# Earlier loads of batch 3, one scaling for both groups of batch 1, and a reordered opening

## The chip, the cores and the metric

The kernel runs on one core of a Trainium2 chip. The time is the device time of one execution in microseconds (us). Five runs of the kernel before gave a median of 313.35 us, from 313.18 to 313.67.

The engines are named as the profile names them: PE (matrix products; PEld are its weight loads), DVE (vector), ACT (scalar functions), POOL and SP. SP computes nothing here and issues most of the DMA transfers; POOL issues those that change the type, and casts v.

## The reference

Two stages. A linear attention over 8 batches, 8 heads, 576 positions and a head size of 64, then a gated feed-forward layer on the 4608 tokens that come out of it (width 512, hidden width 1536):

```python
q_s = np.exp(q - max(q, axis=-1));  q_s = q_s / sum(q_s, axis=-1)
k_s = np.exp(k - max(k, axis=2));   k_s = k_s / sum(k_s, axis=2)
kv  = einsum('bhsd,bhse->bhde', k_s, v)
x   = einsum('bhsd,bhde->bhse', q_s, kv)      # then (batch, position, head*64)
g   = x @ w_gate
out = (g * sigmoid(g) * (x @ w_val)) @ w_out
```

Inputs and output are float32. The kernel computes in bfloat16 with float32 sums. It takes no maximum, and it divides by the sum of k after the product K^T V rather than before.

## The kernel before

**Attention.** A batch is worked on as two groups G of four heads. For each group: `exp_of` (ACT) makes eq and ek; `norm_sum` and `norm_mul` (DVE) divide eq by its row sums and give qs; qs is turned, giving qt, either by PE (`turn_pe`, then a copy `turn_out`) for batches 0 and 1, or by a DMA transpose on SP's queue (`turn_dma`, L178) for the others. `cast_v` (POOL, L122) writes v in bfloat16 beside a column of ones, so `kv_mm` (L187), 72 products of 64x64 over both groups, gives K^T V and the sum of k at once. Scaling by the reciprocal of that sum gives kn. The x product (`x_mm` for batch 0, `x_and_next_kv` for the others, L242) multiplies kn with qt, and ACT and DVE copy the result from PSUM into xt (L256, L257).

**Feed-forward.** The tokens go in chunks: 576 of batch 0, then 448, then 512 each. `m_unit` makes 128 of the 1536 hidden values for a chunk: eight (or sixteen) products with w_gate and w_val (L281), a silu on ACT (L288) and a product on DVE (L289). `o_mm` multiplies hidden values with w_out (L306) for 128 tokens in twelve steps m; `o_out` copies the result to an o_sb buffer and stores it in two halves (L299) on SP's queue.

**What sets the order.** The order on each engine is written out by hand, and every engine works through its own list in order. PSUM has eight banks, handed out as they come free. The tiles for loaded q, k and v have three buffers each (`ld`), ek, eq, qs and qt two (`at`), o_sb five. A load into a buffer in use waits at the head of SP's queue, with everything behind it.

**Around the change.** In the opening, batch 0 is turned, multiplied and copied while the first weight slices are on their way. Then come the loads of batches 1 and 2 on SP, then the first chunk's twelve `m_unit`, and then a stretch in which `o_mm` of the first tokens fills PE between the steps of batch 1's attention. There K^T V of batch 1 has two banks for each group, and each group's half is scaled by its own reciprocal (L482) and product (L483):

```python
for G in range(NG):
    kv_mm(1, G, kv[G], 0)
    for g in range(2):
        kvr = at.tile([128, 1], FP32, tag=f"kvr{g}", name="kvr")
        nc.vector.reciprocal(out=kvr, in_=kv[G][g][:, 64:65])
        nc.vector.tensor_scalar_mul(kn[:, g, G], kv[G][g][:, 0:64], kvr)
```

Later batches use two banks for both groups (columns 0 and 256 of each) and `scale_both` (L227, L228). Batch 3's loads stand at the end of this stretch, behind the stores of the first four outputs and ahead of batch 2's first transpose. Batch 2's x product follows in the second chunk, after its eleventh `m_unit`, together with batch 3's K^T V.

Of the kernel before, what the change touches and what calls it, by code (L numbers as in the profile page):

```python
# [8 lines left out]
FP32 = mybir.dt.float32  # L9
BF16 = mybir.dt.bfloat16  # L10
# [5 lines left out]
def kernel(  # L16
# [10 lines left out]
    nc = tc.nc  # L27
# [8 lines left out]
    NG = H // 4  # L36
# [5 lines left out]
    at = ctx.enter_context(tc.tile_pool(name="at", bufs=2))  # L42
# [4 lines left out]
    def bank(name):  # L47
        return psp.tile([128, 512], FP32, tag="ps", name=name)
# [16 lines left out]
    def head_ap(src, b, G, t0=0, t1=T):  # L65
        return bass.AP(
            tensor=src.tensor,
            offset=src[b, 4 * G].offset + 64 * t0,
            ap=[[T * 64, 128], [2 * HSTR, 2], [1, (t1 - t0) * 64]],
        )  # L70

    def load(what, src, b, G, pieces=((0, T),), after=None):
        t_ = ld.tile([128, 2, T * 64], FP32, tag=what, name=what)
        raw[what, b, G] = t_
        last = None
        for t0, t1 in pieces:
            last = nc.sync.dma_start(out=t_[:, :, 64 * t0:64 * t1], in_=head_ap(src, b, G, t0, t1))  # L77
            if after is not None:
                tc.add_manual_dep(last.ins, after.ins.name, SYNC, reason="order of loads")
                after = None  # L80
        return last

    def load_kv(b):
        for G in range(NG):
            load("k", k, b, G)
            load("v", v, b, G)
# [17 lines left out]
    def copy(eng, out, in_):  # L104
        if eng is nc.scalar:
            nc.scalar.copy(out=out, in_=in_)  # L106
        else:
            eng.tensor_copy(out=out, in_=in_)  # L108
# [3 lines left out]
    st = {}  # L112

    def exp_of(what, b, G, pieces=((0, T),)):
        s = st.setdefault((b, G), {})
        e = s["e" + what] = at.tile([128, T, 2, 64], BF16, tag="e" + what, name="e" + what)
        src = raw[what, b, G].rearrange("p h (t d) -> p t h d", d=64)
        for t0, t1 in pieces:
            nc.scalar.activation(out=e[:, t0:t1], in_=src[:, t0:t1], func=AF.Exp)  # L119
# [34 lines left out]
    def turn_pe(b, G, i):  # L154
        s = st[b, G]
        if i == 0:
            s["qt"] = at.tile([128, T, 128], BF16, tag="qt", name="qt")
        t0, t1 = BANKS[i]
        tp = s["tp", i] = psp.tile([128, 1024], BF16, tag="ps", name="tp")
        for t in range(t0, t1):  # L160
            j = t - t0
            nc.tensor.transpose(  # L162
                out=tp[:, j * 128:(j + 1) * 128], in_=s["qs"][:, t, :], identity=ident
            )

    def turn_out(b, G, i, eng):
        s = st[b, G]
        t0, t1 = BANKS[i]
        copy(
            eng,  # L170
            s["qt"][:, t0:t1, :],
            s["tp", i][:, 0:(t1 - t0) * 128].rearrange("p (t c) -> p t c", c=128),
        )
# [8 lines left out]
    def kv_mm(b, G, kv, c):  # L182
        ek = st[b, G]["ek"]
        for t in range(T):
            for g in range(2):
                for h in range(2):
                    nc.tensor.matmul(  # L187
                        out=kv[g][HALF[h], c:c + 65], lhsT=ek[HALF[g], t, h, :],
                        rhs=vbs[G][HALF[g], t, h, :],
                        start=(t == 0), stop=(t == T - 1),  # L190
                    )

    def x_mm(b, G, i):
        s = st[b, G]
        t0, t1 = BANKS[i]
        xp = [bank("xp") for _ in range(2)]
        for g in range(2):
            for h in range(2):
                r = slice(64 * h, 64 * h + 64)
                nc.tensor.matmul(  # L200
                    out=xp[h][64 * g:64 * g + 64, 0:64 * (t1 - t0)],
                    lhsT=s["kn"][r, g, :],
                    rhs=s["qt"][r, t0:t1, 64 * g:64 * g + 64],
                    start=True, stop=True,
                )
        return xp

    def x_out(b, G, i, xp, engs=(nc.scalar, nc.vector)):
        t0, t1 = BANKS[i]
        n = 64 * (t1 - t0)  # L210
        c0 = b * S + 64 * t0
        for h in (h for h in range(2) if engs[h] is not None):
            copy(engs[h], xt[:, 2 * G + h, c0:c0 + n], xp[h][:, 0:n])
# [1 line left out]


    def kv_both(b):
        kv = st["kv", b] = [bank("kv") for _ in range(2)]
        for G in range(NG):
            kv_mm(b, G, kv, 256 * G)  # L220

    def scale_both(b):
        kn = st["kn", b] = at.tile([128, 2, NG, 64], BF16, tag="kn2", name="kn2")
        for g in range(2):
            kv = st["kv", b][g].rearrange("p (G c) -> p G c", c=256)
            kvr = at.tile([128, NG], FP32, tag=f"kvrr{g}", name="kvr")
            nc.vector.reciprocal(out=kvr, in_=kv[:, :, 64])  # L227
            nc.vector.tensor_mul(kn[:, g], kv[:, :, 0:64], kvr.to_broadcast([128, NG, 64]))  # L228
# [72 lines left out]
    def o_mm(j, o_ps=None, m0=0, m1=MT):  # L301
        if o_ps is None:
            o_ps = bank("o_ps")
        r0 = (j * 128) % RING
        for m in range(m0, m1):
            nc.tensor.matmul(  # L306
                out=o_ps, lhsT=hr[:, m, r0:r0 + 128], rhs=wo[:, m, :],
                start=(m == 0), stop=(m == MT - 1),
            )
        return o_ps  # L310

    def o_out(j, o_ps, eng=nc.vector):
        o_sb = osb.tile([128, 512], FP32, tag="o_sb", name="o_sb")
        copy(eng, o_sb, o_ps)
        store(j, o_sb)
# [20 lines left out]
    with tc.manual_schedule():  # L336
# [50 lines left out]
        def kv_first(G, t0=0, t1=T):  # L387
            s = st[0, G]
            if t0 == 0:
                s["kv"] = [bank("kv") for _ in range(2)]  # L390
            for t in range(t0, t1):
                for g in range(2):
                    for h in range(2):
                        nc.tensor.matmul(
                            out=s["kv"][g][HALF[h], 0:64], lhsT=s["ek"][HALF[g], t, h, :],
                            rhs=v16[G][HALF[g], h, 64 * t:64 * t + 64],
                            start=(t == 0), stop=(t == T - 1),
                        )

        def scale_first(G, eng1):  # L400
            s = st[0, G]
            kn = s["kn"] = at.tile([128, 2, 64], BF16, tag="kn1", name="kn1")
            nc.scalar.mul(kn[:, 0, :], s["kv"][0][:, 0:64], s["kvr"][:, 0:1])
            if eng1 is nc.scalar:
                nc.scalar.mul(kn[:, 1, :], s["kv"][1][:, 0:64], s["kvr"][:, 1:2])
            else:
                nc.vector.tensor_scalar_mul(kn[:, 1, :], s["kv"][1][:, 0:64], s["kvr"][:, 1:2])
# [12 lines left out]
        key_sum(1)  # L420
        scale_first(0, nc.scalar)
        turn_pe(0, 1, 0)
        turn_out(0, 1, 0, nc.vector)
        xp0 = x_mm(0, 0, 0), x_mm(0, 0, 1)
        turn_pe(0, 1, 1)
        turn_out(0, 1, 1, nc.vector)
        kv_first(1, *BANKS[0])
        kv_first(1, *BANKS[1])
        x_out(0, 0, 0, xp0[0], (nc.scalar, None))
        x_out(0, 0, 1, xp0[1], (nc.scalar, None))  # L430
        scale_first(1, nc.vector)
        x_out(0, 0, 0, xp0[0], (None, nc.scalar))
        x_out(0, 0, 1, xp0[1], (None, nc.vector))
        xp1 = x_mm(0, 1, 0), x_mm(0, 1, 1)
        x_out(0, 1, 0, xp1[0])
        x_out(0, 1, 1, xp1[1])
# [7 lines left out]
        for what, src in (("q", q), ("k", k), ("v", v)):  # L444
            for G in range(NG):
                load(what, src, 2, G)

        for m in range(MT):
            m_unit(0, S, m, by_group=(m == 0))
# [21 lines left out]
        turn_pe(1, 1, 1)  # L471
        turn_out(1, 1, 0, nc.scalar)
        turn_out(1, 1, 1, nc.vector)
        kv = [[bank("kv") for _ in range(2)] for _ in range(NG)]
        p3 = o_mm(3, m1=6)
        o_out(2, p2)
        kn = st["kn", 1] = at.tile([128, 2, NG, 64], BF16, tag="kn2", name="kn2")
        for G in range(NG):
            kv_mm(1, G, kv[G], 0)
            for g in range(2):  # L480
                kvr = at.tile([128, 1], FP32, tag=f"kvr{g}", name="kvr")
                nc.vector.reciprocal(out=kvr, in_=kv[G][g][:, 64:65])  # L482
                nc.vector.tensor_scalar_mul(kn[:, g, G], kv[G][g][:, 0:64], kvr)  # L483
        exp_of("q", 2, 0)
        o_mm(3, p3, m0=6, m1=9)
        x_and_next_kv(1, with_kv=False)
        o_mm(3, p3, m0=9)
        o_out(3, p3)
        exp_of("q", 2, 1)
        norm_sum(2, 0)  # L490
# [3 lines left out]
        exp_of("k", 2, 1)  # L494
        cast_v(2, 0)
        cast_v(2, 1)
        load_kv(3)
        turn_dma(2, 0)

        chunks = [(S, 448)] + [(c, 512) for c in range(1024, n_tok, 512)]  # L500
        for ci, (c0, n) in enumerate(chunks):
            b = ci + 2
# [84 lines left out]
```

The softmax here doesn't subtract the row's maximum and nothing guards it: scores larger than these inputs give would overflow.

## Time and profile before

| | |
|---|---|
| median of the runs | 313.35 us |
| the profiled execution | 313.33 us |
| its span, first to last instruction | 311.2 us |
| PE, DVE, ACT, POOL busy | 302.0, 161.2, 146.7, 33.2 us |
| granted PE clock | 1.00 |
| DMA moved, mean rate | 45.78 MB, 147 GB/s |

The profile is one execution. Busy time is given by engine; instructions that only wait, branch or issue a DMA don't count as busy, and those of a queue are named with a q (SPq). A row of the timeline gives start and length in us, engine, line, operation, what is written and read, and in brackets how long the engine was idle before it and what it then waited for. The chain is followed back from the last instruction, at each step to what released it. Lengths of matmuls include their pipeline, so the distance between starts says more than the length.

### The profile page before, as it was taken

What the parts mean: (1) busy time and instruction counts of PE and PEld (TensorE: products, weight loads), DVE (VectorE), ACT (ScalarE), POOL (GpSimd) and SP (SyncE); (2) the same over time, 40 slices, a digit from 0 to 9 for tenths busy, and PEclk for the clock granted to TensorE, in tenths of its full rate; (3) what the DMA queues carried; (4) which work ended last, traced back from release to release, by engine and by line L of the source; (5) the groups of instructions that cost most, each with busy time, mean ns of one, the idle gap of its engine ahead of it and who ended that gap; (6) DMA issues with size and microseconds to landing.
All of it is one profiled execution on the core that took longest, in us unless ns stands there. A gap on an engine that the chain in (4) does not pass through costs nothing.

```text
span 311.2 us, 5454 instructions
## 1 busy us (share of the span) xinstructions
PE 302.0 (97%) x2182; PEld 149.4 (48%) x2182; DVE 161.2 (52%) x277; ACT 146.7 (47%) x215; POOL 33.2 (11%) x39
## 2 busy tenths in 40 slices
PE   6889999999999999999999999999999999999994
PEld 2567845545444444454444444444444444444442
DVE  3834478936763567355836492639354333333321
ACT  5843478794764465547364637455143113312300
POOL 2960021420200110002000200000000000000000
PEclk9999999999999999999999999999999999999999
DMA  7999999899355906491629253605310302020134
GB/s 279 181 193 204 277 386 389 292 236 379 106 100 150 373 17 132 91 376 61 143 62 354 110 108 69 189 0 106 65 42 0 70 8 60 3 67 8 25 70 103
DMA packets 41690, 45.78 MB, mean 147 GB/s; under 512 B 18496, under 2 KB 25664, under 8 KB 41664
## 3 DMA queue, kind: packets, MB, share of 16 engines
q1 hardware_dynamic: 32752, 39.99, 43.5%
q0 software_dynamic: 8752, 5.31, 12.0%
q8 instruction: 17, 0.28, 0.4%
q10 hardware_dynamic: 160, 0.13, 0.1%
q14 instruction: 9, 0.07, 0.1%
HBM read 37.75 MB, written 9.44 MB: 152 GB/s over the span
## 4 chain that ended last, share of the span: by engine, by line
PE 93%; DMA 4%; POOL 1%; issue 0%; SPq 0%; DVE 0%
PE g_ps L281 30%; PE u_ps L281 30%; PE o_ps L306 29%; DMA wg<-in_moe_w_gate_dram 2%; DMA k<-in_k_dram 2%; PE xp L242 2%; PE kv L187 2%; PE o_ps L326 1%; POOL v L344 0%; PE tp L162 0%; POOL v L341 0%; POOL wg L94 0%; POOL wv L94 0%; SPq L77 0%; DVE o_sb L330 0%
## 5 line engine op out<-in xcount | busy, mean ns | idle before, releaser
L288 ACT ACTIVATE sg<-g_ps 128x512 bf16<-128x512 f32 (+2 forms) x120 | 64.7, 555 | 134.9 <-PE g_ps L281 133.1
L289 DVE TENSOR_TENSOR hr<-sg,u_ps 128x512 bf16<-128x512 bf16 (+2 forms) x120 | 74.2, 630 | 89.0 <-PE u_ps L281 82.5
L281 PE MATMUL g_ps<-xt,wg 128*128 128x512 bf16 (+2 forms) x480 | 111.4, 358 | 0.9 <-DMA wg<-in_moe_w_gate_dram 0.9
L281 PE MATMUL u_ps<-xt,wv 128*128 128x512 bf16 (+2 forms) x480 | 111.3, 358 | 0.0
L306 PE MATMUL o_ps<-wo,hr 128*128 128x512 bf16 x420 | 93.9, 379 | 0.0
L281 PEld LDWEIGHTS <-wv 128*128 128x128 bf16 x480 | 46.9, 98 | 46.4
L281 PEld LDWEIGHTS <-wg 128*128 128x128 bf16 x480 | 46.2, 98 | 46.5 <-DMA wg<-in_moe_w_gate_dram 1.2
L306 PEld LDWEIGHTS <-hr 128*128 128x128 bf16 x420 | 40.9, 98 | 48.5
L108 DVE COPY o_sb<-o_ps 128x512 f32<-128x512 f32 x33 | 22.5, 681 | 39.2 <-PE o_ps L306 39.2
L122 POOL CAST vb<-v 128x1152 bf16<-128x1152 f32 x14 | 18.3, 1308 | 134.6 <-DMA v<-in_v_dram 123.0
L133 DVE TENSOR_REDUCE rs<-eq 128x18 f32<-128x1152 bf16 (+2 forms) x18 | 21.7, 1215 | 12.9 <-ACT eq L119 12.9
L147 DVE TENSOR_TENSOR qs<-eq,rr 128x1152 bf16<-128x1152 bf16 (+2 forms) x18 | 21.7, 1216 | 0.1
L119 ACT ACTIVATE eq<-q 128x1152 bf16<-128x1152 f32 (+2 forms) x18 | 18.3, 1052 | 4.0 <-DMA q<-in_q_dram 3.9
L119 ACT ACTIVATE ek<-k 128x1152 bf16<-128x1152 f32 (+2 forms) x17 | 18.1, 1102 | 0.3 <-DMA k<-in_k_dram 0.2
L288 ACT ACT_TABLE_LOAD x12 | 15.4, 1283 | 0.2
L119 ACT ACT_TABLE_LOAD x11 | 14.1, 1283 | 0.2
L256 ACT CAST xt<-xp 128x512 bf16<-128x512 f32 x14 | 7.9, 587 | 4.5 <-PE xp L242 4.4
L371 PE MATMUL idle<-zero 128*128 128x512 bf16 x20 | 6.3, 467 | 3.0 <-DVE rs L133 1.8
L257 DVE CAST xt<-xp 128x512 bf16<-128x512 f32 x14 | 9.0, 683 | 0.0
L242 PE MATMUL xp<-qt,kn 64*64 64x512 bf16 (+1 forms) x112 | 7.2, 293 | 0.0
L187 PEld LDWEIGHTS <-ek 64*64 64x64 bf16 x504 | 6.3, 107 | 1.7 <-ACT qt L106 0.4
L187 PE MATMUL kv<-vb,ek 64*64 64x65 bf16 x504 | 6.8, 194 | 0.0
(45 smaller groups left out, 63.3 us busy)
## 6 DMA issues: line engine op xcount, KB each, us to landing
q<-in_q_dram SPq DMA_DIRECT2D x16, 576.0 KB, 5.5
out_dram<-o_sb SPq DMA_DIRECT2D x70, 128.0 KB, 2.4
k<-in_k_dram SPq DMA_DIRECT2D x15, 576.0 KB, 7.3
v<-in_v_dram SPq DMA_DIRECT2D x14, 576.0 KB, 8.5
wo<-in_moe_w_out_dram POOLq DMA_DIRECT2D x4, 384.0 KB, 14.3
wg<-in_moe_w_gate_dram POOLq DMA_DIRECT2D x2, 384.0 KB, 10.6
wv<-in_moe_w_val_dram POOLq DMA_DIRECT2D x2, 384.0 KB, 11.8
wg<-in_moe_w_gate_dram POOLq DMA_DIRECT2D x2, 256.0 KB, 7.7
```

Of the source, the lines that this page charges most:

```text
L108: eng.tensor_copy(out=out, in_=in_)
L119: nc.scalar.activation(out=e[:, t0:t1], in_=src[:, t0:t1], func=AF.Exp)
L122: return nc.gpsimd.tensor_copy(out=vbs[G][:, :, :, 0:64], in_=raw["v", b, G].rearrange("p h (t d) -> p t h d", d=64),)
L133: i = nc.vector.reduce_sum(out=rs[:, 2 * t0:2 * t1], in_=eq2[:, 2 * t0:2 * t1, :], axis=mybir.AxisListType.X)
L147: last = eng.tensor_mul(qs[:, t0:t1, :].rearrange("p t (h d) -> p (t h) d", d=64), eq2[:, 2 * t0:2 * t1, :], s["rr"][:, 2 * t0:2 * t1].to_ ...
L187: nc.tensor.matmul(out=kv[g][HALF[h], c:c + 65], lhsT=ek[HALF[g], t, h, :], rhs=vbs[G][HALF[g], t, h, :], start=(t == 0), stop=(t == T - 1),)
L242: nc.tensor.matmul(out=o[h][HALF[g], c:c + 64 * (t1 - t0)], lhsT=kn[HALF[h], g, G, :], rhs=qt[G][HALF[h], t0:t1, 64 * g:64 * g + 64], star ...
L257: nc.vector.tensor_copy(out=xt[:, 2 * G + 1, c0:c0 + 512], in_=main[G][1])
L281: nc.tensor.matmul(out=gu[a][i][:, 0:w_], lhsT=(wg, wv)[a][:, kk, ms], rhs=xt[:, kk, c:c + w_], start=(kk == 0), stop=(kk == KT - 1),)
L288: nc.scalar.activation(out=sg[:, 0:w_], in_=g_ps[:, 0:w_], func=AF.Silu)
L289: nc.vector.tensor_mul(hr[:, m, r:r + w_], sg[:, 0:w_], u_ps[:, 0:w_])
L306: nc.tensor.matmul(out=o_ps, lhsT=hr[:, m, r0:r0 + 128], rhs=wo[:, m, :], start=(m == 0), stop=(m == MT - 1),)
```

## The change

There are three edits. In the opening, the two PE transposes of group 1 stand together ahead of the x product of group 0, and the copies of that product to xt are dealt out differently: group 0's first half (h = 1) goes to DVE instead of ACT, and ACT's copy of the second bank pair (h = 0) stands behind the scaling of group 1 instead of ahead of it. In the stretch after the first chunk, K^T V of batch 1 is put into two banks for both groups and scaled by `scale_both`, and five instead of three `o_mm` steps of the fourth output stand between it and the x product. Three of batch 3's four loads move from behind the first outputs' stores to a place right behind batch 2's loads.

```diff
     def kv_both(b):
-        kv = st["kv", b] = [bank("kv") for _ in range(2)]
+        if ("kv", b) not in st:
+            st["kv", b] = [bank("kv") for _ in range(2)]
         for G in range(NG):
-            kv_mm(b, G, kv, 256 * G)
+            kv_mm(b, G, st["kv", b], 256 * G)
...
         turn_pe(0, 1, 0)
+        turn_pe(0, 1, 1)
         turn_out(0, 1, 0, nc.vector)
+        turn_out(0, 1, 1, nc.vector)
         xp0 = x_mm(0, 0, 0), x_mm(0, 0, 1)
-        turn_pe(0, 1, 1)
-        turn_out(0, 1, 1, nc.vector)
         kv_first(1, *BANKS[0])
         kv_first(1, *BANKS[1])
         x_out(0, 0, 0, xp0[0], (nc.scalar, None))
-        x_out(0, 0, 1, xp0[1], (nc.scalar, None))
         scale_first(1, nc.vector)
-        x_out(0, 0, 0, xp0[0], (None, nc.scalar))
-        x_out(0, 0, 1, xp0[1], (None, nc.vector))
+        x_out(0, 0, 0, xp0[0], (None, nc.vector))
+        x_out(0, 0, 1, xp0[1])
...
             for G in range(NG):
                 load(what, src, 2, G)
+        load("k", k, 3, 0)
+        load("v", v, 3, 0)
+        load("k", k, 3, 1)
...
-        kv = [[bank("kv") for _ in range(2)] for _ in range(NG)]
+        st["kv", 1] = [bank("kv") for _ in range(2)]
         p3 = o_mm(3, m1=6)
         o_out(2, p2)
-        kn = st["kn", 1] = at.tile([128, 2, NG, 64], BF16, tag="kn2", name="kn2")
-        for G in range(NG):
-            kv_mm(1, G, kv[G], 0)
-            for g in range(2):
-                kvr = at.tile([128, 1], FP32, tag=f"kvr{g}", name="kvr")
-                nc.vector.reciprocal(out=kvr, in_=kv[G][g][:, 64:65])
-                nc.vector.tensor_scalar_mul(kn[:, g, G], kv[G][g][:, 0:64], kvr)
+        kv_both(1)
+        scale_both(1)
         exp_of("q", 2, 0)
-        o_mm(3, p3, m0=6, m1=9)
+        o_mm(3, p3, m0=6, m1=11)
         x_and_next_kv(1, with_kv=False)
-        o_mm(3, p3, m0=9)
+        o_mm(3, p3, m0=11)
         o_out(3, p3)
...
         cast_v(2, 1)
-        load_kv(3)
+        load("v", v, 3, 1)
         turn_dma(2, 0)
```

## The prediction

> **What bounds the kernel now.** I read the page's busy times and chain first, then the waits, then the timeline of each engine around the three places that the diff touches. PE is busy for nearly the whole span, and the chain that ended last is PE almost throughout.
>
> ```profile
> PE 302.0 (97%) x2182; PEld 149.4 (48%) x2182; DVE 161.2 (52%) x277; ACT 146.7 (47%) x215; POOL 33.2 (11%) x39
> PE 93%; DMA 4%; POOL 1%; issue 0%; SPq 0%; DVE 0%
> ```
>
> So an edit pays only if it closes a gap in PE's stream, and costs only if it opens one. From the timelines of PE and of its weight loads, these are the gaps near the edits (start, length, what, idle before it):
>
> ```profile
> 17.27 1.15 PE L281 MATMUL g_ps<-xt,wg 128*128 128x320 bf16 x8 [0.92 <-DMA wg<-in_moe_w_gate_dram]
> ...
> 50.65 0.11 PEld L242 LDWEIGHTS <-kn 64*64 64x64 bf16 x4 [0.42 <-DVE kvr L482]
> 50.98 0.11 PEld L242 LDWEIGHTS <-kn 64*64 64x64 bf16 x2 [0.23 <-DVE kn L483]
> 51.38 0.35 PEld L242 LDWEIGHTS <-kn 64*64 64x64 bf16 x10 [0.29 <-DVE kn L483]
> ```
>
> The first is the opening: unit m=1 of the first chunk waits for a slice of w_gate. The other three are batch 1's x product waiting for the scaled K^T V. From 52.4 us to the last chunks single matmuls follow each other at their own pace (0.19 or 0.216 us), so nothing else is there to win. The other reading that matters is SP's queue, and who needs it (SP, then PE, then the group of the transposes: shortest, median, longest in ns):
>
> ```profile
> 48.58 8.36 SPq L299 DMA_DIRECT2D out_dram<-o_sb  x8
> 58.72 0.58 SPq L77 DMA_DIRECT2D v<-in_v_dram  x1
> 59.41 8.09 SPq L178 DMA_TRANSPOSE qt<-qs  x2
> ...
> 70.02 0.41 PE L242 MATMUL xp<-qt,kn 64*64 64x512 bf16 x4
> ...
> L178 SPq DMA_TRANSPOSE qt<-qs x12: 1275/1343/4252, 59.4 to 217.9; - x12
> ```
>
> The two transposes of batch 2 land at 68.48 and 69.50; PE uses them at 70.02 and 70.58. That is the tightest thing downstream: 1.5 and 1.1 us.
>
> **Part 1, the opening.** Nothing is added; four transposes move ahead of the x product, and one copy of 128x320 goes from ACT (0.42) to DVE (0.49). The moved transposes need the second half of qs, written by DVE until 12.19. PE would reach them at about 12.1, so it stands until 12.25; four at 0.056 plus the 0.1 us that PE takes here between shapes put the x product at 12.56 instead of 12.18. The transposes no longer stand behind it, so the K^T V of group 1 begins at about 13.0 (12.94 before) and its scalings at about 13.5, as now. After them DVE has four copies (0.49, 0.42, 0.49, 0.42, overlapping by some 0.05) instead of three: it ends near 15.55 instead of 15.07. Unit m=0, which ended at 16.35, ends by 16.8 at worst. What hides this is the 0.92 us wait: m=1's w_gate slice lands at 17.22 whatever PE did, and m=2's w_val slice lands at 20.11, 0.1 us before its use at 20.22. Price: 0, and 0.45 us without that cover. A gain here is excluded for the same reason.
>
> **Part 2, scaling both groups at once.** Before: four reciprocals and four multiplications, two of each now, of twice the width. The same operations stand in the trace for the later batches:
>
> ```profile
> L227 DVE RECIPROCAL kvr<-kv x12: 159/162/165, 61.6 to 200.6; 128x2 f32<-128x2 f32 x12
> L228 DVE TENSOR_TENSOR kn<-kv,kvr x12: 291/292/292, 61.8 to 200.8; 128x128 bf16<-128x128 f32 x12
> L482 DVE RECIPROCAL kvr<-kv x4: 157/157/169, 49.7 to 50.8; 128x1 f32<-128x1 f32 x4
> L483 DVE TENSOR_SCALAR kn<-kv,kvr x4: 283/284/284, 49.9 to 51.0; 128x64 bf16<-128x64 f32 x4
> ```
>
> Start to end the old chain took 49.66 to 51.32 = 1.66 us; the new one, as at 61.63 to 62.52, 0.89. But it starts later. The page "PSUM — Partial Sum Buffer" of the Trainium skill (section "PSUM bank collisions raise a hardware error") says that no two engines may be on the same bank and group of 32 partitions at once, other columns included. Now both groups share a bank, so DVE can't begin on group 0 while group 1 multiplies; the row at 49.66 shows it doing so in separate banks. Without the rule the new chain would run 49.66 to 50.55. With it, it starts 0.05 after the last kv matmul ends (49.96), so 50.01 to 50.90. I take 50.90.
>
> **Part 3, five o_mm steps instead of three ahead of the x product.** PE leaves the kv matmuls at 49.90; five steps (0.226 + 4 x 0.216 = 1.09) and 0.09 for the change of shape bring it to 51.08, after kn (50.90 + 0.06): all three waits go. The x product then runs without gaps: at 70.02 its groups take about 0.22 each and its tails 0.18, so 0.62, to 51.70 (51.78 before, from an earlier start). One o_mm step is left behind it, 0.22: PE is at m_unit at 51.92. Before, 1.00 us after the first x matmul gaps and three steps had already covered the copies to xt; now the copies are late next. ACT's starts 0.45 after the first x matmul (51.10 against 50.65), so at 51.53; 0.59 long plus 0.06 until PE sees it gives 52.18. DVE's (0.68) gives 52.27, for the second matmul at 52.37. The second pair lands at 52.8 to 52.9, used at 52.94 and 53.13. So m_unit starts at 52.18, against 52.435: **0.25 us won**. PE loses nothing in work: the same 12 o_mm steps. Bounds: 0.52 if the copies were not late (the gaps summed), 0 if DVE or ACT were 0.25 later.
>
> ACT and DVE come out of this 0.26 to 0.29 later than now (their copies start at 51.53 instead of 51.10), and PE 0.25 earlier. First silu at 57.05 becomes 57.31, its bank free at 57.9; the fifth unit wants it at 58.49 - 0.25 = 58.24. That leaves 0.3 us of cover; were it gone, each 0.1 costs 0.1.
>
> **Part 4, the loads.** Of batch 3's four loads, k0, v0 and k1 move ahead of eight stores; v1 stays behind them. SP is one queue, and each of its DMAs reuses the completion semaphore of the eighth before it: the stores at 50.55, 52.05, 53.56, 55.01 and 56.48 each start 0.02 after the landings at 50.53, 52.03, 53.54, 54.99 and 56.46. With that rule and a load's 1.47 us when queued (landings 52.03, 53.54, 54.99, 56.46), the new order is:
> k0 issues at 48.58 and v0 at 49.1 (buffers free at 48.26 and 48.39), landing 57.9 and 59.4. k1 needs the buffer that ACT's exp of batch 2's k0 frees, now near 54.9; SP stands there from 49.6 to 55.0. Behind it wait the eight stores, v1 and the transposes; nobody needs the stores (five o_sb buffers, the sixth output is at 83.8). Five stores issue to 57.4; the last three wait for k0, v0 and k1 to land: 57.9, 59.4, 60.9. v1 issues at 61.5, the first transpose at 62.0 instead of 59.41.
>
> Is that a delay? "DMA: Bandwidth & Descriptors" (section "Anatomy of one DMA — SWDGE (gpsimd) path") says that a semaphore wait is served on the issuing sequencer, and that the DMA engines only consume what is queued. Taken alone that speaks against the change: everything behind k1 slips by 55.0 - 48.58 = 6.4 us, the second transpose to 75.9, and PE stands from 70.3 for 5.6 us (318.7). The rows say otherwise. The DMA share of 48.8 to 52.5 is 1.05, and with k0 and v0 queued the engines have data to 59.4 and then k1: they never starve. The bytes are the same, so: k1 60.9, eight stores of 0.31 to 63.4, v1 64.9. Before, v1's turn in the queue ended at 64.81 + 1.5 = 66.3 and the transposes landed 2.2 and 3.2 later; so now 67.1 and 68.1, against needs of 69.8 and 70.3. The long issues (3.74 and 4.25) stood behind three or four queued loads, against 1.34 when free; behind one load I take them as shorter. Price 0. Upper bound: both as long as before, 62.0 + 3.74 + 0.05 + 4.25 = 70.1, landing 2.0 later (67.50 to 69.50) at 72.1: 1.8 us of stall. The casts of v and exps of k for batch 3 get their data 2.6 to 3.9 us earlier, but ACT's stand behind PE-paced silus (61.80) and POOL's behind the kv matmuls at 60.1: no gain on PE.
>
> **Sum.** 0 - 0.25 + 0 + 0. The profiled execution took 313.33 (span 311.2 and 2.1 around it); its median over runs is 313.35, so 313.08 there is **313.1** as a median. A measurement of this kernel can't tell differences under about 0.2%, 0.63 us, so I call it no change.
>
> **Rivals.** (a) The chain is as long as ever: DVE starts late or the copies take the whole gain, so PE starts m_unit at 52.43 and the time is 313.35. For it: the copies already bind in my sum. Against: kn and PE arrive 0.18 apart in the right order. (b) Slower: SP's stand at k1. The transposes of batch 2 land too late for the x product. It decides from a second landing past 70.3, gives back the gain at 70.55, and is over 0.63 us slower past 71.2; at the bound of 72.1 the time is 313.35 - 0.25 + 1.8 = 314.9. For it: issues of up to 4.25 us under load. Against: less is queued ahead of them than before. (c) Slower from the opening: DVE's fourth copy makes m=0 end past 17.2. It needs 0.45 us more than I worked out; at 1.4 us more the price is 0.95, and the time 314.3.
>
> **How the numbers follow.** My sum 0.60 (own range 312.8 to 313.4), (a) 0.12, (b) 0.20, of which 0.05 stays within 0.63 us, (c) 0.05; 0.03 for a gain over 0.63, more than the gaps hold. Faster 0.03; same 0.60 + 0.12 + 0.05 = 0.77; slower 0.15 + 0.05 = 0.20. The range takes in the 0.52 bound and noise below, 312.7, and above it part of (b) and (c), up to 314.3; left out are the worst of (b) and a little below, some 0.15.
>
> **What would show it.** Part 1: the wait before m=1 stays, shortened to 0.5 to 0.9, and PE's start at 17.27 stands. Parts 2 and 3: no PE wait on kn, the second chunk's first g_ps near 52.2 with a short wait on ACT's xt copy. Part 4: stores from 55 us, first transpose issued near 62, landings before 69.8, PE without a gap at 70. Wrong if PE waits on qt, if the silus hold PE at 58, or if the w_gate wait is gone.

## The result, and the profile after

The changed kernel takes **312.13 us** in the median of 23 runs (311.89 to 314.36); the kernel before, run beside it on the same chip, 313.45 in 44 runs (312.30 to 316.68). The ratio is 0.9965, with an interval of 0.995 to 0.998: faster by 0.35%, some 1.1 us. The forecast was 313.1, no change, with a range down to 312.7. The gain is real, and most of it was not in the sum.

The profiled execution took 312.81 us with a span of 310.7, against 313.33 and 311.2. First the page's busy times and the chain that ended last:

```profile
PE 302.8 (97%) x2182; PEld 149.9 (48%) x2182; DVE 162.0 (52%) x274; ACT 146.2 (47%) x214; POOL 32.4 (10%) x39
PE 93%; DVE 3%; ACT 1%; DMA 1%; issue 0%
```

PE is the bound as before. DVE has three working instructions fewer. Next, PE's timeline around the two edits in its stream (start, length, what; in brackets its idle time):

```profile
14.12 0.66 PE L282 MATMUL g_ps<-xt,wg 128*128 128x320 bf16 x4
...
16.09 1.14 PE L282 MATMUL g_ps<-xt,wg 128*128 128x320 bf16 x8
...
44.02 0.68 PE L162 MATMUL tp<-ident,qs 128*128 128x128 bf16 x9 [0.16 <-DVE qs L147]
...
46.98 0.68 PE L162 MATMUL tp<-ident,qs 128*128 128x128 bf16 x9 [0.56 <-DVE qs L147]
...
49.62 1.25 PE L307 MATMUL o_ps<-wo,hr 128*128 128x512 bf16 x5
50.80 0.69 PE L243 MATMUL xp<-qt,kn 64*64 64x512 bf16 x16
51.42 0.39 PE L307 MATMUL o_ps<-wo,hr 128*128 128x512 bf16 x1
51.89 0.54 PE L282 MATMUL g_ps<-xt,wg 128*128 128x448 bf16 x2
```

Unit m=1 starts at 16.09 with no wait, since its slice of w_gate landed at 14.91 in this execution. The x product of batch 1 runs as one stretch; the three waits for kn are gone. The second chunk's first product starts at 51.89 instead of 52.44, after the copies to xt (ACT's first from 51.25, 0.59 long). And PE now waits twice for qs of batch 1, at 44.02 and 46.98, where most of the early start is given back. The rows of qs and of the cast of v that overlaps it, before and after:

```profile
42.86 1.36 DVE L147 TENSOR_TENSOR qs<-eq,rr 128x1152 bf16<-128x1152 bf16 x1
42.91 2.31 POOL L122 CAST vb<-v 128x1152 bf16<-128x1152 f32 x1 [19.06 <-DMA v<-in_v_dram]
...
41.61 1.14 POOL L122 CAST vb<-v 128x1152 bf16<-128x1152 f32 x1 [19.05 <-DMA v<-in_v_dram]
41.67 2.29 DVE L147 TENSOR_TENSOR qs<-eq,rr 128x1152 bf16<-128x1152 bf16 x1
```

Before, DVE started first and POOL's cast took long; in the profile after, the cast started 0.06 us ahead and qs took 0.93 us longer. This is a matter of the execution: of the other profiles below only one, without opening and 3 more, has it (qs 2.22 us); in the rest qs takes 1.36.

SP's queue, then the transposes' group:

```profile
47.80 0.41 SPq L77 DMA_DIRECT2D k<-in_k_dram  x1
48.24 0.47 SPq L77 DMA_DIRECT2D v<-in_v_dram  x1
54.64 0.37 SPq L77 DMA_DIRECT2D k<-in_k_dram  x1
55.05 5.48 SPq L300 DMA_DIRECT2D out_dram<-o_sb  x8
60.62 0.53 SPq L77 DMA_DIRECT2D v<-in_v_dram  x1
61.27 4.86 SPq L178 DMA_TRANSPOSE qt<-qs  x2
```
```profile
L178 SPq DMA_TRANSPOSE qt<-qs x12: 1273/1316/3462, 61.3 to 217.3; - x12
```

That is the forecast schedule, within 0.9 us: the stores stand behind k1, the transposes of batch 2 are issued at 61.27 and 64.84, land at 66.64 and 68.14, and PE takes them at 69.47 and 70.03 without a gap.

Where did the time go, by marks on PE and the end of the span:

| | first o_mm | first K^T V of batch 1 | second chunk's first g_ps | last matmul | end |
|---|---|---|---|---|---|
| before | 38.84 | 49.13 | 52.44 | 307.05 | 311.19 |
| after | 37.65 | 48.88 | 51.89 | 306.50 | 310.67 |

From the second chunk's first product to the last matmul both take 254.62 us. So this pair of profiles differs by 0.30 in the scaling stretch (3.31 against 3.01) and 0.25 ahead of it, nothing else. On this pair alone one would call Part 4's zero right. The runs say otherwise: before goes from 312.3 to 316.7, while 17 of the changed kernel's 23 runs lie within 312.5, and the execution profiled after took 0.7 us more than the median. Low granted clocks do not explain the spread: of 67 runs of the kernel before beside the first experiments, the 60 with a mean clock of 0.997 or more still go from 312.3 to 315.6, and the changed kernel's such runs from 311.9 to 313.4. One execution of each does not show what tells the two apart.

### The profile page after: what moved, and what is told of

Read it like the earlier page. It is cut to its first block, busy times and chain, and to the rows that moved or that the text cites. A ratio compares the mean times of both kernels' runs of the same rounds, so it can differ in the third digit from the quotient of the medians.

```text
span 310.7 us, 5449 instructions
## 1 busy us (share of the span) xinstructions
PE 302.8 (97%) x2182; PEld 149.9 (48%) x2182; DVE 162.0 (52%) x274; ACT 146.2 (47%) x214; POOL 32.4 (10%) x39
## 4 chain that ended last, share of the span: by engine, by line
PE 93%; DVE 3%; ACT 1%; DMA 1%; issue 0%
PE g_ps L282 30%; PE u_ps L282 30%; PE o_ps L307 27%; PE kv L187 2%; PE xp L243 1%; PE idle L372 1%; DMA q<-in_q_dram 1%; DVE qs L147 1%; DVE rs L133 1%; PE o_ps L327 1%; PE tp L162 1%; ACT eq L119 1%; ACT L119 0%; PE xp L200 0%; PE kv L395 0%
## 5 line engine op out<-in xcount | busy, mean ns | idle before, releaser
L122 POOL CAST vb<-v 128x1152 bf16<-128x1152 f32 x14 | 17.5, 1248 | 136.9 <-DMA v<-in_v_dram 127.4
L147 DVE TENSOR_TENSOR qs<-eq,rr 128x1152 bf16<-128x1152 bf16 (+2 forms) x18 | 22.9, 1283 | 0.1
L372 PE MATMUL idle<-zero 128*128 128x512 bf16 x20 | 7.8, 555 | 2.7 <-DVE rs L133 1.4
```

What stands on the lines that cost most here:

```text
L122: return nc.gpsimd.tensor_copy(out=vbs[G][:, :, :, 0:64], in_=raw["v", b, G].rearrange("p h (t d) -> p t h d", d=64),)
L147: last = eng.tensor_mul(qs[:, t0:t1, :].rearrange("p t (h d) -> p (t h) d", d=64), eq2[:, 2 * t0:2 * t1, :], s["rr"][:, 2 * t0:2 * t1].to_ ...
L372: i = nc.tensor.matmul(out=idle, lhsT=zero[:, 0:128], rhs=zero, start=True, stop=True)
```

## The experiments

All ratios are to the kernel before, run beside them. The runs were made in five groups (four, four, four, three, two), each on one chip; from group to group the chip can differ, so there the ratios compare better than the medians. "Front" is the start of the second chunk's first g_ps in the run's profile, "rest" the time from there to the last matmul, "tail" from the start of the last matmul to the end of the span.

| run | median (range) | ratio, interval | front | rest | tail |
|---|---|---|---|---|---|
| before again | 312.96 (312.11 to 315.57) | 1.0000, 0.9979 to 1.0021 | 52.07 | 255.31 | 4.11 |
| opening alone | 312.81 (312.25 to 315.70) | 0.9999, 0.9980 to 1.0018 | 51.70 | 256.55 | 4.09 |
| loads alone | 312.82 (312.41 to 313.97) | 0.9972, 0.9956 to 0.9987 | 52.98 | 254.62 | 4.21 |
| scaling alone | 313.36 (312.30 to 314.48) | 0.9993, 0.9969 to 1.0017 | 52.15 | 254.61 | 4.37 |
| k1 ahead of v0 | 312.87 (312.22 to 313.49) | 0.9984, 0.9966 to 1.0002 | 52.05 | 254.62 | 4.20 |
| k1 last | 315.19 (314.79 to 318.42) | 1.0081, 1.0050 to 1.0111 | 51.21 | 257.49 | 4.18 |
| without opening | 313.52 (312.71 to 314.95) | 1.0008, 0.9993 to 1.0024 | 51.50 | 254.62 | 5.08 |
| without loads | 313.76 (313.03 to 316.14) | 1.0029, 1.0009 to 1.0048 | 51.15 | 255.93 | 5.07 |
| without opening, 3 more | 312.33 (311.60 to 313.24) | 0.9968, 0.9955 to 0.9981 | 52.31 | 254.62 | 4.13 |
| changed, 1 less | 313.21 (312.67 to 314.71) | 0.9996, 0.9979 to 1.0013 | 52.73 | 254.62 | 5.08 |
| without loads, 3 more | 313.39 (312.19 to 316.74) | 0.9995, 0.9975 to 1.0015 | 51.66 | 255.62 | 4.13 |
| changed, 3 more | 312.07 (311.83 to 313.27) | 0.9973, 0.9959 to 0.9986 | 51.13 | 254.62 | 4.19 |
| k1 stays behind | 312.82 (312.23 to 314.57) | 0.9982, 0.9963 to 1.0000 | 51.12 | 254.84 | 4.12 |
| k1 last of all | 315.13 (313.96 to 318.60) | 1.0076, 1.0044 to 1.0107 | 51.35 | 256.56 | 4.15 |
| k alone ahead | 312.72 (311.91 to 314.30) | 0.9984, 0.9957 to 1.0011 | 53.01 | 254.62 | 4.18 |
| changed, 3 more, again | 312.23 (311.86 to 312.57) | 0.9964, 0.9945 to 0.9983 | 51.26 | 254.62 | 4.21 |
| k alone ahead, again | 312.37 (311.82 to 313.48) | 0.9958, 0.9937 to 0.9980 | 50.74 | 254.94 | 4.21 |

**Which part brings it.** The first four runs: no edit, and each of the three edits alone as the diff above has it (the loads alone: the `load` lines; the scaling alone: `kv_both`, `scale_both` and the `o_mm` steps; the opening alone: the copies and transposes).

> The kernel before, unchanged, as a kernel of its own: how far its executions spread, and a second profile of it. Theory S (the sum of the prediction: only the scaling stretch gains, and what else differs between the two profiles is when the opening's DMAs arrive in that execution): no difference, ratio 1.000, and in the profile the second w_gate slice lands anywhere from 14.9 to 17.2 us, with PE's wait at unit m=1 following it. Theory T (batch 2's transposes often land too late for PE in the kernel before, and the earlier loads cure that): this profile shows PE waiting on qt near 70 us, or the second transpose landing within 0.5 us of its use. Theory O (the reordered opening itself brings the rest): the profile again shows a wait of about 0.9 us at m=1.

> Only the opening's reordering, loads and scaling as before. S: no difference (within 0.2 us). T: no difference. O: some 0.9 us faster, and the second w_gate slice lands by 15 us.

> Only the three loads of batch 3 moved ahead of the stores. S: no difference (within 0.2 us). T: 0.5 to 1.0 us faster in the median, with less spread, and transposes landing more than 1.5 us ahead of their use near 70 us. O: no difference.

> Only the scaling of batch 1 for both groups at once, with five o_mm steps ahead of the x product. S: 0.25 to 0.3 us faster; x product without gaps, m_unit's first product 0.2 to 0.3 after the last o_mm step. T: 0.25 to 0.3 faster too, but with the spread of the kernel before, and PE now reaches batch 2's x product 0.3 us earlier, so waits there on qt eat part of it. O: 0.25 to 0.3 faster.

The loads alone come out faster, by 0.28% or 0.9 us, and only they are clear of zero. The sum of the prediction gave them nothing, so theory S is refuted, and so is the opening as the carrier of the gain (theory O). Theory T, late transposes in the kernel before, had forecast this number. But before again shows no wait on qt: the second transpose lands at 69.51 and is used at 70.82, 1.3 us of cover. With the loads alone it lands at 69.72 and is used at 71.13, hardly better covered (1.4). The profile of the kernel before, taken again, shows what the first one did not. ACT's timeline, then PE's:

```profile
62.00 1.28 ACT L119 ACT_TABLE_LOAD   x1
63.29 1.16 ACT L119 ACTIVATE ek<-k 128x1152 bf16<-128x1152 f32 x1
65.59 1.16 ACT L119 ACTIVATE ek<-k 128x1152 bf16<-128x1152 f32 x1 [1.13 <-DMA k<-in_k_dram]
66.77 1.28 ACT L288 ACT_TABLE_LOAD   x1
68.06 2.37 ACT L288 ACTIVATE sg<-g_ps 128x448 bf16<-128x448 f32 x5
```
```profile
66.53 0.92 PE L281 MATMUL g_ps<-xt,wg 128*128 128x448 bf16 x4
67.29 0.92 PE L281 MATMUL u_ps<-xt,wv 128*128 128x448 bf16 x4
68.66 0.92 PE L281 MATMUL g_ps<-xt,wg 128*128 128x448 bf16 x4 [0.45 <-ACT sg L288]
```

The exp of batch 3's second load of k (k1) stands on ACT ahead of the silus. k1 landed at 65.56; the exp, the table load and one silu follow, and only that silu frees the bank that PE wants for its next g_ps, at 68.66: 3.10 us behind the landing. In the first profile of before the same load landed at 64.81, 0.03 before ACT asked for it. Its rows from the same views, ACT's and then PE's next g_ps:

```profile
63.66 2.34 ACT L119 ACTIVATE ek<-k 128x1152 bf16<-128x1152 f32 x2
66.01 1.28 ACT L288 ACT_TABLE_LOAD   x1
67.31 1.85 ACT L288 ACTIVATE sg<-g_ps 128x448 bf16<-128x448 f32 x4
68.41 0.92 PE L281 MATMUL g_ps<-xt,wg 128*128 128x448 bf16 x4
```

Two exps without a gap, and no wait on PE.

**Theory K: k1's landing.** Two runs move only k1 within `load_kv(3)` of the kernel before, everything still behind the stores; two more leave one part out of the changed kernel.

```diff
-        load_kv(3)          # k0, v0, k1, v1
+        load("k", k, 3, 0)
+        load("k", k, 3, 1)  # k1 ahead of v0; in the other run it stands last
+        load("v", v, 3, 0)
+        load("v", v, 3, 1)
```

> The kernel before with one swap: batch 3's second k load ahead of its first v load, all four still behind the stores. Theory K (ACT's exp of batch 3's second k waits for that load, the silus behind it come late, and PE waits at the second chunk's unit m=10 for a bank; the stall ends 3.1 us after that load lands): the load lands near 63.3 instead of 64.8 to 66.4, no PE gap at m=10, and the median is 0.4 to 0.8 us faster, as with the loads alone. Theory T (the transposes): no difference, since the transposes stand behind the same bytes.

> The kernel before with batch 3's second k load last of its four, still ahead of the transposes. K: it lands near 67.5, so PE goes on at m=10 near 70.6 instead of 68.2, a stall of some 2.4 us; the median is 1.5 to 2.2 us slower than before (which has 0 to 1.9 of that stall itself). T: no difference.

> The changed kernel with the opening as before: loads and scaling only. K together with the prediction's scaling gain: as fast as the changed kernel, 312.1, ratio 0.996 to 0.997. If the opening adds something once the loads are early: 0.2 us or more slower than the changed kernel.

> The changed kernel with the loads of batch 3 as before: opening and scaling only. K: the second k load lands when it did, so what PE wins in the scaling stretch it waits at m=10; the median is that of before within 0.2 us, and the profile shows a gap at m=10 whenever the load lands after 65.0. S (the gains simply add): 0.3 us faster.

k1 last costs 0.8%, although the transposes stand behind the same bytes: that is against theory T. k1 one place earlier lands at 63.50; its profile has no stall, and the long end of the range is gone (nothing above 313.49). Its gain, 0.3 us by the medians and 0.5 by the ratio (0.4 to 0.8 forecast), is just not clear of zero. The last two both came out too long, the one without the opening by 1.4 us: its profile has no stall at all, and yet its time is that of the kernel before. The table shows where it sits, in the tail.

**Theory F: the instruction fetch.** In both of these the last stores land late. The DMA issues in the last stretch, from the last matmul on, of the run without the opening (KB each, median us from issue to landing):

```profile
q14 instruction: 2, 0.02, 1.2%
...
out_dram<-o_sb SPq DMA_DIRECT2D x1, 32.0 KB, 3.0
out_dram<-o_sb ACTq DMA_DIRECT2D x1, 32.0 KB, 3.1
```

Elsewhere these two take 2.0 and 2.2. Two packets of 8192 bytes of the queue "instruction" start here at 308.51 and 308.65, while the stores' 512-byte packets are moving (308.17 to 309.23). In the kernel before one such packet comes at 305.90, ahead of the last stores, and the other at 309.82, when their last packets are through (309.58). By the queue's name these packets bring the engines their own instructions, so the moment at which one falls should hang on how many instructions come before it: DVE's stream holds, waits included, 457 instructions in the kernel before, 455 in the changed one, and 454 in the two runs whose last stores land late (each trace records four fewer: 453, 451, 450). The test changes the number and nothing of the work:

```diff
         for vb in vbs:
             nc.vector.memset(vb[:, :, :, 64:65], 1.0)
+        for _ in range(3):
+            nc.vector.memset(vbs[0][:, 0:1, 0:1, 64:65], 1.0)
```
```diff
-        for vb in vbs:
-            nc.vector.memset(vb[:, :, :, 64:65], 1.0)
+        nc.vector.memset(vbs[0][:, :, :, 64:65], 1.0)
...
         w_dma = [wo_slice(m0, 3) for m0 in (0, 3, 6, 9)]
+        nc.gpsimd.memset(vbs[1][:, :, :, 64:65], 1.0)
```

> The changed kernel with the opening as before (as in the run that came out at 313.52 where 312.1 was expected), and with three one-element memsets more on DVE in the first 2 us, where DVE waits for the first loads; they write ones where ones stand. DVE's instruction stream has 457 instructions with them, as the kernel before has, and 454 without. Theory F (instruction fetch): in the build with 454 an 8 KB packet of the instruction queue falls between the packets of the last stores and makes them land 1 us later (last matmul to end of span 5.08 instead of 4.1 to 4.2 us). With 457 it falls some 1.1 us before the last matmul, as in the kernel before: 4.15 us from last matmul to end, and 312.5 (313.52 less 0.95; down to 312.1 if the opening is worth nothing at all). Rival N: the fetch is harmless and the missing 1.4 us is what the opening edit brings in company of the two other parts: 313.5, and 5.1 us from last matmul to end.

> The changed kernel with one DVE instruction fewer: the memset of ones in the second buffer of v goes to POOL, behind the issues of the weights (that buffer is first read at about 20 us). DVE's stream has 454 instructions instead of 455. Theory F: the packet of the instruction queue moves from 1.1 us before the last matmul to 2.4 us behind it, between the last stores' packets: 5.1 us from last matmul to end instead of 4.17, and 313.1. Rival N: 312.1 to 312.2, 4.2 us from last matmul to end.

> The changed kernel with batch 3's loads as before (the run that came out at 313.76), and the same three memsets more on DVE (457 instructions instead of 454). Theory F: 4.15 us from last matmul to end instead of 5.07, and 312.8. What is left against the changed kernel (312.1) is then the price of k1's late landing, theory K: 0.7 us in the median, with a stall of PE at the end of the silus of the second chunk of batch 0 and 1 that obeys 'landing of the second load of k + 3.1 us', 0 to 2 us by execution, and a wide spread of times. Rival N: 313.8.

> The changed kernel with the same three memsets more on DVE (458 instructions instead of 455): the control. Theory F: the packet stays about 1.1 us before the last matmul, as in the kernel before with 457 and in the runs with 458; nothing moves: 312.1 to 312.2, 4.17 us from last matmul to end. If the memsets themselves had a price or a gain, it would show here.

Three idle memsets make the kernel without the opening 1.2 us faster (313.52 to 312.33, tail 5.08 to 4.13). One instruction moved from DVE to POOL makes the changed kernel 1.1 us slower by the medians, 0.7 to 1.0 by the ratios (tail 4.17 to 5.08). Three more on the changed kernel do nothing. The same stretch of the padded run without the opening:

```profile
q14 instruction: 1, 0.01, 1.0%
...
out_dram<-o_sb SPq DMA_DIRECT2D x1, 32.0 KB, 2.0
out_dram<-o_sb ACTq DMA_DIRECT2D x1, 32.0 KB, 2.2
```

So F holds as far as these builds go: the tail follows the count, and the late stores the packets. It explains nothing of the gain: before and after have the same tail (4.14 and 4.17). It only spoilt two experiments, and those that follow are padded. The run without loads, padded, was to be 312.8 and came out at 313.39: K's price in that company is 1.3 us by the medians, 0.7 by the ratios (0.9995 against 0.9973), where 0.7 was taken.

**Is it k1 alone?** k1 ahead of v0 had gained less than the loads together (0.9984 against 0.9972), so three runs split the loads of the changed kernel (padded).

```diff
         load("k", k, 3, 0)
         load("v", v, 3, 0)
-        load("k", k, 3, 1)
...
+        load("k", k, 3, 1)   # ahead of v1 (k1 stays behind), or behind it (k1 last of all)
         load("v", v, 3, 1)
```
```diff
         load("k", k, 3, 0)
-        load("v", v, 3, 0)
         load("k", k, 3, 1)
...
+        load("v", v, 3, 0)
         load("v", v, 3, 1)
```

> The changed kernel (with the three memsets more on DVE) in which the second load of k of batch 3 alone stays behind the output stores, as before: k0 and v0 ahead of the stores, then stores, k1, v1, transposes. k1 is issued about 60.5 us and lands at 64.5 to 65.5, a little ahead of the kernel before (64.8 to 66.4), as k0 and v0 are out of its way. Theory K (k1's exp on ACT stands ahead of the silus; PE goes on at landing + 3.1 us): PE stalls 0 to 1.2 us in the second chunk's unit m=10, by execution: 312.6 to 313.0. Rival R (the loads' gain is spread: v0 for POOL, k0 for ACT, shorter queue at the transposes): half or more of the gain stays, most of it with k0 and v0: 312.1 to 312.4, no stall at m=10.

> The same with k1 behind v1: stores, v1, k1, transposes. k1 lands 1.5 us later than in the previous run, at 66 to 67. Theory K: PE goes on at 69.1 to 70.1 where it would have been there at about 67.3: 1.8 to 2.8 us, 314.0 to 314.8. Rival R: v1 lands earlier, k1's exp is needed only at about 70.4 for batch 3's matmuls: 312.1 to 312.6.

> The same with the two loads of k ahead of the stores and both loads of v behind them. k1 lands at about 60. Theory K: no stall at m=10, as in the changed kernel: 312.1. Rival R: v0 is cast by POOL some 3 us later, and half or more of the gain is gone: 312.6 or more.

With k1 left behind, the median is where theory K had it (312.6 to 313.0), but the ratio, 0.9982 against 0.9973 and 0.9964 of the padded changed kernel, leaves half of the gain or more, and the intervals overlap. This run alone does not decide: with k0 and v0 out of its way k1 lands at 64.14, ahead of every landing of the old order, and its profile stalls by only 0.22. With k1 last the kernel is 0.76% slower than before (ten of its sixteen runs lie between 313.96 and 315.40, the others above 317). ACT and PE of that last run:

```profile
66.12 1.16 ACT L119 ACTIVATE ek<-k 128x1152 bf16<-128x1152 f32 x1 [2.38 <-DMA k<-in_k_dram]
67.30 1.28 ACT L289 ACT_TABLE_LOAD   x1
68.59 2.37 ACT L289 ACTIVATE sg<-g_ps 128x448 bf16<-128x448 f32 x5
```
```profile
66.57 0.92 PE L282 MATMUL u_ps<-xt,wv 128*128 128x448 bf16 x4
69.19 0.92 PE L282 MATMUL g_ps<-xt,wg 128*128 128x448 bf16 x4 [1.70 <-ACT sg L289]
```

Landing at 66.10, PE at 69.19: the same 3.1 us, now with ACT 2.38 and PE 1.70 idle. The third run, the loads of k alone ahead, fell between the theories: 312.72, while its profile had no stall and a late front (53.01), which was late before these loads were issued (first o_mm at 38.93). One profile does not explain a median, so it was run again beside the changed kernel.

> The changed kernel with the three memsets more once more, beside the next run on one chip: 312.1 (0.9973 or a little less of the kernel before); from the first matmul of batch 1's gate product to the last matmul of all 254.6 us.

> Both loads of k ahead of the stores, both of v behind, once more. In its first profile nothing stalled behind the first matmul of batch 1's gate product (254.61 us from there to the last matmul, as in the changed kernel), and what was slow was the stretch ahead of it, which these loads cannot touch. Theory K: the same as the changed kernel beside it within 0.3 us. Rival R (v0 late costs): 0.5 us or more above it.

312.37 against 312.23, 0.14 apart: v0's earlier load brings nothing that can be measured, and k1's brings the gain of the loads. Why the first run of this kernel came out at 312.72 stays open.

**The law in numbers.** PE goes on 3.09 to 3.10 us behind k1's landing wherever it stalls there, and without a stall it would be there 15.90 us behind the front (fitted on before again). What is lost is the difference, if positive; the last column is measured without the landing:

| run | k1 lands | + 3.10 | front + 15.90 | lost by this | rest - 254.62 |
|---|---|---|---|---|---|
| before, first profile | 64.81 | 67.91 | 68.34 | 0 | 0 |
| before again | 65.56 | 68.66 | 67.97 | 0.69 | 0.69 |
| opening alone | 66.43 | 69.53 | 67.60 | 1.93 | 1.93 |
| scaling alone | 64.81 | 67.91 | 68.05 | 0 | -0.01 |
| k1 ahead of v0 | 63.50 | 66.60 | 67.95 | 0 | 0 |
| without loads | 65.27 | 68.37 | 67.05 | 1.32 | 1.31 |
| without loads, 3 more | 65.46 | 68.56 | 67.56 | 1.00 | 1.00 |
| k1 last | 66.88 | 69.98 | 67.11 | 2.87 | 2.87 |
| k1 stays behind | 64.14 | 67.24 | 67.02 | 0.22 | 0.22 |
| k1 last of all | 66.10 | 69.20 | 67.25 | 1.95 | 1.94 |
| after | 60.04 | 63.14 | 67.79 | 0 | 0 |

So in the kernel before, PE went on with the second chunk at the later of two things, its own pace and k1. In the six profiles with the old order of loads and k1 in its old place (before twice, opening alone, scaling alone, and without loads twice) 0 to 1.9 us are lost, 0.8 in the mean; the loads alone gained 0.9. By this law, whatever is won ahead of k1 is lost again while k1 binds. The scaling alone (0.9993) and the opening alone (0.9999) fit that, but do not show it: the interval of the scaling alone also holds the whole 0.3 us, its profile has no stall, and its tail is 0.2 longer (453 instructions in DVE's stream). Nor do the times show that the scaling's 0.3 us count once k1 is out of the way: the loads alone reach 0.9972, the padded changed kernel 0.9973 and 0.9964.

## Why the prediction was wrong

**Part 4, the loads: the step that failed.** It said that batch 3's data come earlier but "ACT's stand behind PE-paced silus (61.80) and POOL's behind the kv matmuls at 60.1: no gain on PE". The exps start when PE's pace lets them, that much was right; what I did not ask is what stands behind the second exp. A silu does, and PE's next bank with it. In the profile that I read, k1 landed at 64.81 with 0.43 us of cover to the point at which PE would stall, and I took the landing of that execution as the landing. In the other profiles with the old order of loads it lands at 64.8 to 66.4. The term that I set to 0 is worth 0.9 us in the loads alone, and 0.7 (ratios) to 1.3 us (medians) in the changed kernel. The sentence "From 52.4 us to the last chunks single matmuls follow each other at their own pace (0.19 or 0.216 us), so nothing else is there to win" was true of one execution in which the cover just held.

**Part 4, SP's queue** was right to within 0.9 us: k1's stand to 54.64 (55.0 forecast), k1's landing 60.04 (60.9), first transpose issued 61.27 (62.0), landings 66.64 and 68.14 (67.1 and 68.1). That the landings fit so well is in part luck: the sum counts from 66.3 as the end of v1's turn before, and v1 landed at 67.53 there. **Rival (b)**, transposes too late, did not happen in the changed kernel. Its condition is near, though: in the run with k alone ahead, again, the front was as early as 50.74, the second transpose landed at 69.14, and PE took it at 69.18, 0.3 us later than its pace (0.56 us from the first use to the second elsewhere, 0.86 here). It is what binds next when the front is faster.

**Parts 2 and 3** were right: the new chain starts once the last K^T V product of both groups is done and takes 49.73 to 50.63, 0.90 us where 0.89 was taken from the later batches; the waits for kn are gone, the copies to xt are late next, and 0.3 us are won in this stretch where 0.25 were forecast; every run with the edit has 3.01 us from the first K^T V product to the second chunk (3.13 in one), every run without it 3.30 or 3.31.

**Part 1**: the x product started at 12.60 (12.56 forecast), unit m=0 was through at 16.09, where 16.8 was the worst case, and the price of 0 stands: alone it measured 0.9999, and taken out of the padded kernel 0.9968 against 0.9973. Its cover was misjudged. The slice of w_gate that I said lands "at 17.22 whatever PE did" landed at 14.91 in the profile after, and at 15.2 to 17.5 in the eight runs of the first two groups, with and without the edit. So the wait before m=1 was gone after, which had been named as a sign of being wrong; the landing removed it, and landings ahead of 16 us came with and without the edit. "A gain here is excluded" does not follow from a landing that moves by 2.5 us; a gain of up to some 0.3 us is neither shown nor refuted.

**Sum.** 0.25 forecast and 0.3 found in the profiles, 0.7 to 1.3 missed, against 1.1 us measured between the two kernels (ratio 0.9965). A gain of this size had been given 3 chances in 100, because all gaps of that one profile together held less.

## What to carry to other kernels

For every load that an in-order engine consumes, write down not only whether it was on time in the profile but by how much, and what stands behind the consumer on that engine; a cover of 0.4 us on a landing that scatters by 1.6 us is no cover. If repeated times scatter more than the stages do, look for such a landing first, and expect that gains ahead of it may measure as nothing until it is moved. When an experiment misses by about a microsecond, compare the tails before forming a theory: a build that differs by one instruction can end differently.

## What the runs showed of the hardware

**Packets of the queue "instruction" among the last stores can lengthen a kernel's end.** In the three builds with 454 DVE instructions (without opening, without loads, changed with 1 less) two 8 KB packets start some 2.4 and 2.5 us behind the last matmul, between the last stores' packets; the stores then take 3.0 us to land instead of 2.0, and the tail is 5.1 us instead of 4.1 or 4.2. In the other profiles one packet comes, at 2.5 us or later, when the stores' packets are through or nearly so, and the stores land as usual (in scaling alone too, whose tail of 4.37 stays open). The Trainium skill's page "Runtime: NRT & Kernel Launch" (section "Instruction fetch mechanics") says that a sequencer fetches its next page by its own DMA queue and that crossing a boundary is mostly hidden. That it fetches during the run agrees with the packets seen; at the kernel's end the cost was not hidden, 0.9 us of tail. The changed kernel is one DVE instruction from that edge. That these packets are DVE's is inferred from their moving with DVE's count alone; no record names the engine.

**Landings scatter from execution to execution.** The second w_gate slice landed at 17.22 and 16.13 in the two profiles of the kernel before, at 16.83 and 14.79 in the two with k alone ahead, and anywhere from 14.8 to 17.5 us over all; k1 from 64.8 to 66.4 with the old order. What sets them within that span was not tried, and the chips differed too.

**A vector product and a cast on POOL that overlap: the later one took longer.** In 17 of the 19 profiles DVE's first product qs of batch 1 started ahead of POOL's cast of v; it took 1.36 us and the cast 1.2 to 2.3. In the other two the cast started first and took 1.14, and the product 2.29 and 2.22.
